# The last half tile of a mixture-of-experts layer as float32 products in two column halves, and the tokens' products without their split

## The chip, the cores and the metric

The program runs on one core of a Trainium2 chip. The metric is the device time of one execution in microseconds (us). TensorE is called PE here, its weight loads PEld, VectorE DVE, ScalarE ACT, GpSimd POOL, and SyncE, which issues most DMAs, SP.

## The reference

Eight batches of 576 tokens go through an attention with 32 memory slots per head, and the result through a layer with eight experts, of which each token uses the one with the highest score.

```python
a = softmax(phi); k_m = a^T k; v_m = a^T v              # 8 batches, 8 heads, 576 tokens, 32 slots, 64 wide
x = softmax(q k_m^T / 8) v_m                            # tokens: [4608, 512]
expert = argmax(norm(x) @ norm(expert_emb).T / tau)     # one of 8
gate = softmax(logits)[expert]
out[token] = gate * (relu(x @ w1[expert]) @ w2[expert]) # 512 -> 1024 -> 512, float32
```

## The kernel before

Float32 accuracy is wanted. A product of two float32 operands that is to run in PE's quick format (float32r) is written as three: each operand is split into a high part and the rest, and high*high, high*low and low*high are added in PSUM. Names ending in h and l are such parts: `wh`, `wl` of the second layer's weights, `gh`, `gl` of the first layer's, `hh`, `hl` of the hidden activations, `vh`, `vl` of the tokens' value weights, and the two `aT` tiles of a batch's transposed attention weights. Other matmuls (`acc`, `pg`, `ts`, `tl`) run on unsplit float32.

A batch nearly always has one expert for all its tokens; `batch(b)` assumes that of the batch's chosen expert, and `rest` handles the other tokens, of which there are none here. `batch(b)` runs the first layer (`first`: 2 halves of 288 tokens by 8 blocks of hidden units, six matmuls each into a PSUM tile `ph` of which there are four buffers, tag "mm", shared with `py`, `pg` and one `tl`) and the second (`second`: tiles of 128 tokens at T0 = 0, 128, 256, 384, 448, 24 matmuls of 512 columns each into `py`). 576 is four and a half times 128, so the fifth tile overlaps the fourth by 64 rows, and only its last 64 rows are written out. After each `ph`, ACT writes `hh` and DVE writes `hl`; between them ACT and DVE split the next weights (`split_w`, with `wl` mostly on POOL).

While `batch(b)` runs, the attention of batch b+1 is woven in between its matmuls: `weigh` (scores transposed, `sc`, then softmax on DVE and ACT), `divide`, `turn` (weights transposed back, `ta`, and split into `aT`), `attend` (the tokens' products with `vh` and `vl` into `po`, with logits beside them), `choose` (the batch's expert, `key`), and then `late`: flags, norms and gates, some 26 small DVE operations and an exponential on ACT. Where a step stands is decided while the program is written, by `run`: it keeps planned times of PE, DVE and ACT (`plan`), and lets a step go once its inputs are due and neither DVE nor ACT is planned more than `slack` ahead of PE. The engines then work through their own instructions in the order written. `choose` also sets the loads of w1 and w2 going on SP, since only then the expert is known.

Batch 0's attention has nothing to be woven into; it is written out by hand at the start (`moe_linformer`) and is followed by batch 1's `te`, `acc`, `tf`, `ts`, `tl` and then `project(0)` (`pg`, `gh`, `gl`) and `first(0)`.

Of the kernel before, what the change touches and what calls it, by code (L numbers as in the profile page):

```python
# [26 lines left out]
T0 = (0, 128, 256, 384, 448)  # L27
# [21 lines left out]
class Tokens:  # L49
# [43 lines left out]
    def turn(self, p):  # L93
        k, nc, b = self.k, self.nc, self.b
        ah, al = k.aT[b % 2]
# [5 lines left out]
        o = 0 if p < 2 else 64  # L101
        g, to = slice(gs[0], gs[-1] + 1), slice(T0[ti[0]] + o, T0[ti[-1]] + P)
        nc.scalar.copy(ah[:, g, to], t[:, :, o:])
        nc.vector.tensor_tensor(out=al[:, g, to], in0=t[:, :, o:], in1=ah[:, g, to].bitcast(F32), op=ALU.subtract)  # L104
        n = 4 if p < 2 else 1
        pe = k.plan("PE", 0.11 * max(n, 2))
        k.end["aT", b, p] = k.plan("DVE", 0.15 + 0.135 * n, k.plan("ACT", 0.2 + 0.1 * n, pe))

    def attend(self, *ti, pt=None):

        k, nc, b = self.k, self.nc, self.b
        ah, al = k.aT[b % 2]
        for i in ti:
            self.po[i] = po = (pt or self.pt)([P, NC * (D + E)], f"po{b}_{i}")
            to = slice(T0[i], T0[i] + P)
            for g in range(NG):
                w = slice(g * (P + E), (g + 1) * (P + E))
# [13 lines left out]
        k.end["po", b, ti[-1]] = k.plan("DVE", 0.35 + 0.18 * len(ti), pe)  # L131
# [86 lines left out]
    def steps(self):  # L218

        k, b = self.k, self.b  # L220
        end = k.end

        def past():

            return b - 2 < k.halved
# [30 lines left out]
class Kernel:  # L256
# [4 lines left out]
    def __init__(self, ctx, tc, phiT, qT, kv, kvt, emb, tau, w1, w2, out):  # L261
# [10 lines left out]
        self.ad = dp.tile([B, P, 2, NG * S], F32, name="ad")  # L272
# [10 lines left out]
        self.sT = st([P, NG, S], F32, name="sT")  # L283
# [3 lines left out]
        self.vh = st([P, NG * (P + E)], F32R, name="vh")  # L287
        self.vl = st([P, NG * (P + E)], F32R, name="vl")
# [3 lines left out]
        self.aT = [[st([P, NG, S], F32R, name=f"aT{i}{k}") for k in range(2)] for i in range(2)]  # L292
# [9 lines left out]
        self.hl = st([P, 8, S], F32R, name="hl")  # L302

# [8 lines left out]
        self.chosen, self.n1, self.n2, self.projected, self.halved, self.halves = set(), 0, 0, 0, -1, 0  # L312
        self.left = None
# [5 lines left out]
    def consts(self):  # L319
# [15 lines left out]
        for x in (self.vh, self.vl):  # L335
            nc.vector.tensor_scalar(
                out=x, in0=self.ident[:, :1].broadcast_to((P, NG * (P + E))), scalar1=0.0, scalar2=None, op0=ALU.mult
            )
# [164 lines left out]
    def scores(self, b, pt, gs=range(NG), products=True):  # L503
# [27 lines left out]
        for g in gs:  # L531
            nc.scalar.copy(self.sT[:, g, 512:], tail[g][:, :64])
            self.plan("ACT", 0.22)
# [3 lines left out]
    def products(self, b):  # L537

        nc = self.nc
        parts = [  # L540
            (slice(64 * k, 64 * k + 64), self.tail[g], slice((P + E) * g + 64 * k, (P + E) * g + 64 * k + D + E))
            for g in range(NG)
            for k in range(2)
        ]
        for h, x, to in parts:
            nc.scalar.copy(self.vh[h, to], x[h, 64:])
            act = self.plan("ACT", 0.23)
        for h, x, to in parts:
            nc.vector.tensor_tensor(out=self.vl[h, to], in0=x[h, 64:], in1=self.vh[h, to].bitcast(F32), op=ALU.subtract)
            self.end["v", b] = self.plan("DVE", 0.24, act)  # L550


    def keep(self, b):

        for k, x in enumerate(self.aT[b % 2]):
            self.nc.sync.dma_start(self.ad[b, :, k], x.rearrange("p g s -> p (g s)").bitcast(F32))
        self.nc.sync.dma_start(self.vd[b].rearrange("p (g k m) -> p g k m", g=NG, k=2), self.vT[b % 2][..., :D])
# [16 lines left out]


# [34 lines left out]
    def first(self, n, at, split):  # L610

        nc = self.nc
        gh, gl, (ah, al) = self.gh, self.gl, at
        free = [0.0] * 4
        for s in range(2):
            to = slice(s * HS, s * HS + HS)
            for f in range(8):
# [11 lines left out]
                free.append(self.plan("DVE", 0.46, self.plan("ACT", 0.42, self.plan("PE", 0.79, free[-4]))))  # L629
# [3 lines left out]
    def second(self, n, gate, put, split):  # L633

        nc = self.nc
        for i in range(NT):
            to = slice(T0[i], T0[i] + P)
            p = self.mm([P, DM], f"py{n}_{i}")
            for f in range(8):
                split(f)  # L640
                for k, (h, w) in enumerate(((self.hh, self.wh), (self.hh, self.wl), (self.hl, self.wh))):
                    nc.tensor.matmul(p, lhsT=h[:, f, to], rhs=w[:, f], start=f == 0 and k == 0, stop=f == 7 and k == 2)  # L642
                pe = self.plan("PE", 0.69)
# [3 lines left out]
            nc.scalar.activation(y, p, AF.Copy, scale=gate[:, i : i + 1])  # L647
            self.plan("ACT", 0.7, pe)
            put(i, y)
            yield  # L650
# [48 lines left out]
    def batch(self, b, attention):  # L699
# [16 lines left out]
        for _ in self.first(b, self.aT[b % 2], split):  # L716
            self.run(attention)
        while self.halves < 8:
            self.split_w(b == 0)
        self.halved = b + 1  # L720
        self.late = True
        self.loads()
        for n, _ in enumerate(self.second(b, self.gate[:, b], self.rows(b), must)):
            if n == 5:
                self.run(attention, lambda: ("gate", b) in self.end)
                if b == B - 1:
                    self.left = self.others()
            self.hold = n >= 16 and b + 1 < B
# [14 lines left out]
    def rows(self, b):  # L743
        def put(i, y):
            o = 0 if i < 4 else 64
            r = b * S + T0[i]
            self.nc.gpsimd.dma_start(self.out[r + o : r + P], y[o:])  # L747
# [13 lines left out]
    def rest(self, fl, ni):  # L761
# [3 lines left out]
        with tc.If(nv > 0, preferred_fallthrough_block=False):  # L765
# [29 lines left out]
            for i in range(NT):  # L795
                nc.gpsimd.iota(
                    tok[:, i : i + 1], pattern=[[0, 1]], base=T0[i], channel_multiplier=1, allow_small_or_imprecise_dtypes=True
                )
            gate = st([P, NT], F32, name="g1")
            ex = st([P, NT], F32, name="e1")  # L800
            ix = st([P, NT], I32, name="ix")
            at, vT = self.aT[0], self.vT[0]

            def put(i, y):
                nc.gpsimd.indirect_dma_start(
                    out=self.out,
                    out_offset=bass.IndirectOffsetOnAxis(ap=ix[:, i : i + 1], axis=0),
                    in_=y,
                    in_offset=None,
                    bounds_check=N - 1,  # L810
# [3 lines left out]
            with tc.For_i(0, nv, 1) as j:  # L814
                b = nc.sync.value_load(tab[:, 0, bass.ds(j, 1)], min_val=0, max_val=B - 1)
                e = nc.sync.value_load(tab[:, 1, bass.ds(j, 1)], min_val=0, max_val=E - 1)
                for k in range(2):
                    nc.sync.dma_start(
                        at[k].rearrange("p g s -> p (g s)").bitcast(F32),
                        self.ad[bass.ds(b, 1), :, k].rearrange("a p s -> (a p) s"),  # L820
                    )
# [7 lines left out]
                bc = st([P, 1], F32, name="bc")  # L829
                nc.vector.tensor_copy(out=ec, in_=ef[:, bass.ds(j, 1)])  # L830
# [3 lines left out]
                nc.vector.scalar_tensor_tensor(out=ix, in0=tok, scalar=bc, in1=ex, op0=ALU.add, op1=ALU.add)  # L834
# [8 lines left out]
                for _ in self.first("r", at, split):  # L843
# [112 lines left out]
```

## Time and profile before

| | |
|---|---|
| median of 3 runs | 481.5 us (479.58 to 481.68) |
| the profiled execution | 479.94 us |
| its span, first to last instruction | 478.1 us |
| PE busy | 451.0 us, 94% |
| DVE, ACT, POOL busy | 262.5, 196.6, 100.4 us |
| mean granted PE clock | 0.978 |

Busy time is the time in which at least one instruction of an engine was under way. Matmuls overlap each other, so the mean duration of one is not what one costs: that is the spacing of their starts, or the length of a row of them divided by their count. The chain of waits goes back from the last instruction, at each step to what released it; read in order of time it tells which engine's work set the end at each moment. "x40" counts instructions as the chip ran them; an unsplit float32 matmul stands there as two (20 `acc` matmuls of the program are x40 in the trace). The granted clock has two levels, 1.00 (2.4 GHz) and 0.50 (1.2 GHz).

### The profile page before, as it was taken

How to read it: one execution, taken by the hardware profiler on the slowest of the kernel's cores; microseconds unless marked ns; L12 is line 12 of the kernel's file. 1: busy time of each engine (PE TensorE's matmuls, PEld its weight loads, DVE VectorE, ACT ScalarE, POOL GpSimd, SP SyncE). 2: the span in 40 equal slices, each digit the busy share in tenths (PEclk: the TensorE clock that was granted, in tenths of full speed). 3: DMA queues.
4: the chain of work that ended last, by engine and by line, in shares of the span. 5: the costliest groups of instructions: out<-in, count | busy, mean ns of one | idle time of the engine just before them, and what ended most of it. 6: DMA issues, size and time to landing. Idle time of an engine off the chain costs nothing.

```text
span 478.1 us, 9454 instructions
## 1 busy us (share of the span) xinstructions
PE 451.0 (94%) x3604; PEld 375.1 (78%) x3604; DVE 262.5 (55%) x875; ACT 196.6 (41%) x479; POOL 100.4 (21%) x108
## 2 busy tenths in 40 slices
PE   3858899999999999999999999999999999999993
PEld 2446598879887798879988798878988798869882
DVE  5463698456846467536856368446756367437100
ACT  4332563157414573137514473236623383126210
POOL 1000041004400170004400071004400062015300
PEclk9966999999999999999999999999999999999998
DMA  8644891199316970299215970199414900094011
GB/s 287 221 186 185 256 368 47 32 347 348 141 45 264 349 254 22 62 385 347 96 45 224 374 268 22 40 344 350 156 44 182 337 2 23 22 338 179 25 45 36
DMA packets 26321, 87.18 MB, mean 182 GB/s; under 512 B 7064, under 2 KB 7064, under 8 KB 24224
## 3 DMA queue, kind: packets, MB, share of 16 engines
q1 hardware_dynamic: 23216, 76.82, 45.1%
q0 software_dynamic: 2944, 9.44, 5.1%
q8 instruction: 30, 0.49, 0.4%
q10 hardware_dynamic: 112, 0.28, 0.2%
q14 instruction: 19, 0.16, 0.1%
HBM read 66.60 MB, written 19.92 MB: 181 GB/s over the span
## 4 chain that ended last, share of the span: by engine, by line
PE 85%; issue 6%; DVE 3%; DMA 2%; POOL 1%; ACT 1%; POOLq 0%; DVEq 0%; ACTq 0%
PE py L642 41%; PE ph L622 21%; PE po L119 6%; PE acc L463 4%; PE pg L600 3%; PE ts L509 2%; PE te L450 2%; PE sc L72 2%; PE ta L100 2%; DMA kx<-kv 1%; DMA kl<-kvt 1%; POOL wl L589 1%; POOL out_dram L747 0%; PE tf_0False L489 0%; PE tl L520 0%
## 5 line engine op out<-in xcount | busy, mean ns | idle before, releaser
L642 PE MATMUL py<-wh,hh 128*128 128x512 f32 x320 | 129.7, 405 | 0.0
L642 PE MATMUL py<-wh,hl 128*128 128x512 f32 x320 | 125.2, 391 | 0.0
L642 PE MATMUL py<-wl,hh 128*128 128x512 f32 x320 | 125.1, 391 | 0.0
L622 PE MATMUL ph<-aT,gh 128*128 128x288 f32 x512 | 104.7, 299 | 1.8 <-DVE gl L604 1.8
L589 POOL TENSOR_TENSOR wl<-w2s,wh 128x512 fp32r<-128x512 f32 x60 | 76.6, 1291 | 122.4 <-ACT wh L580 115.8
L622 PEld LDWEIGHTS ph<-aT,gh 128*128 128x128 f32 x512 | 81.3, 188 | 5.8 <-DVE gl L604 4.8
L647 ACT ACTIVATE ys<-py,gate 128x512 f32<-128x512 f32 x40 | 27.5, 687 | 126.2 <-PE py L642 103.7
L622 PE MATMUL ph<-aT,gl 128*128 128x288 f32 x256 | 75.3, 294 | 0.0
L747 POOL DMA_DIRECT2D out_dram<-ys x40 | 22.1, 552 | 248.9 <-ACT ys L647 165.5
L626 DVE SCALAR_TENSOR_TENSOR hl<-ph,hh 128x288 fp32r<-128x288 f32 x128 | 56.1, 453 | 29.5 <-ACT hh L625 29.1
L642 PEld LDWEIGHTS py<-wh,hl 128*128 128x128 f32 x320 | 60.1, 188 | 13.3
L642 PEld LDWEIGHTS py<-wh,hh 128*128 128x128 f32 x320 | 60.2, 188 | 11.7 <-issue 1.2
L642 PEld LDWEIGHTS py<-wl,hh 128*128 128x128 f32 x320 | 60.3, 188 | 10.3
L625 ACT ACTIVATE hh<-ph 128x288 fp32r<-128x288 f32 x128 | 50.8, 413 | 25.6 <-PE ph L622 25.5
L622 PEld LDWEIGHTS ph<-aT,gl 128*128 128x128 f32 x256 | 48.0, 188 | 0.0
L604 DVE TENSOR_TENSOR gl<-pg,gh 128x512 fp32r<-128x512 f32 x32 | 19.9, 683 | 47.2 <-ACT gh L603 47.2
L119 PE MATMUL po<-vh,aT 128*128 128x136 f32 x160 | 30.1, 287 | 0.8 <-DVE aT L104 0.8
L580 ACT CAST wh<-w2s 128x512 fp32r<-128x512 f32 x50 | 30.5, 614 | 0.0
L119 PEld LDWEIGHTS po<-vh,aT 128*128 128x128 f32 x160 | 28.3, 208 | 2.8 <-DVE aT L104 1.0
L125 DVE TENSOR_REDUCE lg<-po 128x8 f32<-128x16 f32 x40 | 7.0, 175 | 40.6 <-PE po L119 40.6
L119 PE MATMUL po<-vl,aT 128*128 128x136 f32 x80 | 23.3, 291 | 0.0
L77 ACT ACTIVATE ea<-ea 128x512 f32<-128x512 f32 (+1 forms) x24 | 13.4, 560 | 22.4 <-DVE ea L76 22.3
(122 smaller groups left out, 490.8 us busy)
## 6 DMA issues: line engine op xcount, KB each, us to landing
kx<-kv SPq DMA_DIRECT2D x32, 512.0 KB, 7.8
w1s<-w SPq DMA_DIRECT2D x16, 1024.0 KB, 5.4
w2s<-w SPq DMA_DIRECT2D x32, 512.0 KB, 9.1
ad<-aT SPq DMA_DIRECT2D x16, 576.0 KB, 13.0
out_dram<-ys POOLq DMA_DIRECT2D x32, 256.0 KB, 2.3
qt<-qT SPq DMA_DIRECT2D x14, 576.0 KB, 6.4
ex<-phiT SPq DMA_DIRECT2D x16, 288.0 KB, 11.1
kl<-kvt SPq DMA_DIRECT2D x7, 256.0 KB, 8.4
```

The source lines that it names most:

```text
L119: nc.tensor.matmul(po[:, 144 * g : 144 * g + P + E], lhsT=x[:, g, to], rhs=v[:, w], start=n == 0, stop=n == 2)
L463: nc.tensor.matmul(self.acc[32 * i : 32 * i + 32, i], lhsT=self.eT[:, 5 * g + k, 32 * j : 32 * j + 32], rhs=src[:, 4 * g + j], start=k == ...
L580: nc.scalar.copy(h, x)
L589: nc.gpsimd.tensor_tensor(out=l, in0=x, in1=h.bitcast(F32), op=ALU.subtract)
L600: nc.tensor.matmul(ps[g][j], lhsT=vT[r, g, c % 2, i], rhs=self.w1s[r, c, f], start=True, stop=True)
L604: nc.vector.tensor_tensor(out=self.gl[:, g, f], in0=ps[g], in1=self.gh[:, g, f].bitcast(F32), op=ALU.subtract)
L622: nc.tensor.matmul(p, lhsT=w[:, g, fs], rhs=x[:, g, to], start=g == 0 and k == 0, stop=g == 1 and k == 2)
L625: nc.scalar.activation(self.hh[:, f, to], p, AF.Relu)
L626: nc.vector.scalar_tensor_tensor(out=self.hl[:, f, to], in0=p, scalar=0.0, in1=self.hh[:, f, to].bitcast(F32), op0=ALU.max, op1=ALU.subtract)
L642: nc.tensor.matmul(p, lhsT=h[:, f, to], rhs=w[:, f], start=f == 0 and k == 0, stop=f == 7 and k == 2)
L647: nc.scalar.activation(y, p, AF.Copy, scale=gate[:, i : i + 1])
L747: self.nc.gpsimd.dma_start(self.out[r + o : r + P], y[o:])
```

## The change

Four things are changed. The fifth tile holds the last 64 tokens alone. It is computed first in `second`, from unsplit float32: `h4`, a new copy of those 64 tokens' activations that ACT writes in `first` after `hh` and `hl`, is the stationary operand (64 columns of the array), and w2's unsplit columns 0 to 255 go to the array's lower 64 columns and 256 to 511 to its upper 64, as two matmuls of 256 columns. The tokens' products are one float32 matmul each, from `aw` (the unsplit transposed weights) and `vv`. The split into `aT`, still needed by `first`, is made from `aw` by DVE and POOL (`part`), in one pair of tiles and no longer two; `turn` of batch b+1 may therefore come only after `first` of batch b. w2 of the next batch may be loaded once the half tile is computed, and no longer before `second`.

```diff
-T0 = (0, 128, 256, 384, 448)
+T0 = (0, 128, 256, 384, 512)
@@ turn
-        nc.scalar.copy(ah[:, g, to], t[:, :, o:])
-        nc.vector.tensor_tensor(out=al[:, g, to], in0=t[:, :, o:], in1=ah[:, g, to].bitcast(F32), op=ALU.subtract)
...
+        a = k.aw[:, g, to]
+        nc.scalar.copy(a, t)
...
+        k.part(g, slice(to.start, min(to.stop, S)))
@@ attend
-                for n, (x, v) in enumerate(((ah, k.vh), (al, k.vh), (ah, k.vl))):
-                    nc.tensor.matmul(
-                        po[:, 144 * g : 144 * g + P + E], lhsT=x[:, g, to], rhs=v[:, w], start=n == 0, stop=n == 2
-                    )
-            pe = k.plan("PE", 0.68)
+                nc.tensor.matmul(po[:, 144 * g : 144 * g + P + E], lhsT=k.aw[:, g, to], rhs=k.vv[:, g], start=True, stop=True)
+            pe = k.plan("PE", 0.5)
@@ products
+                if g:
+                    self.nc.vector.tensor_copy(out=to, in_=x)
+                else:
+                    self.nc.scalar.copy(to, x)
@@ part (new)
+        self.nc.vector.tensor_copy(out=ah, in_=a)
+        self.nc.gpsimd.tensor_tensor(out=al, in0=a, in1=ah.bitcast(F32), op=ALU.subtract)
@@ first, after hh and hl
+                if s:
+                    nc.scalar.activation(self.h4[:, f], p[:, HS - 64 :], AF.Relu)
+                    free[-1] = max(free[-1], self.plan("ACT", 0.21))
@@ second
-        for i in range(NT):
+        for i in (NT - 1, *range(NT - 1)):
+            half = i == NT - 1
...
+                if half:
+                    for j in range(2):
+                        nc.tensor.matmul(
+                            p[64 * j : 64 * j + 64],
+                            lhsT=self.h4[:, f],
+                            rhs=self.w2s[:, f, d * j : d * j + d],
+                            start=f == 0,
+                            stop=f == 7,
+                        )
...
```

The order of three engines shows where this stands. On PE, the end of `first` and the start of `second` in batch 3, with the scores `sc` of batch 4 between them; before:

```order
L622 MATMUL ph3_17_2761<-aT10_87,gl_95 128x288
L642 MATMUL py3_0_2772<-wh_92,hh_96 128x512
L642 MATMUL py3_0_2772<-wl_93,hh_96 128x512
L642 MATMUL py3_0_2772<-wh_92,hl_97 128x512
L72 MATMUL sc4_0_2776<-ident_116,sT_79 128x128 x4
...
```

and changed:

```order
L623 MATMUL ph3_17_2677<-aT0_84,gl_93 128x288
L649 MATMUL py3_4_2689<-w2s_89,h4_96 64x256 x2
L73 MATMUL sc4_0_2692<-ident_115,sT_79 128x128 x4
L73 MATMUL sc4_1_2701<-ident_115,sT_79 128x128 x4
L73 MATMUL sc4_2_2710<-ident_115,sT_79 128x128 x2
L649 MATMUL py3_4_2689<-w2s_89,h4_96 64x256 x14
L660 MATMUL py3_0_2735<-wh_90,hh_94 128x512
...
```

Sixteen matmuls of the half tile stand where the first tile of 24 began, and the scores go in after the first two of them.

On ACT, the second half of `first` in batch 3, with what each row waits for; before:

```order
L625 ACTIVATE hh_96<-ph3_11_2701 128x288 [waits PE_49]
L580 CAST wh_92<-w2s_91 128x512 [waits DMAHW6_49,Pool_49]
L625 ACTIVATE hh_96<-ph3_12_2712 128x288 [waits PE_49]
L625 ACTIVATE hh_96<-ph3_13_2721 128x288 [waits PE_49]
L625 ACTIVATE hh_96<-ph3_14_2732 128x288 [waits PE_49]
```

and changed:

```order
L626 ACTIVATE hh_94<-ph3_11_2611 128x288 [waits PE_49]
L633 ACTIVATE h4_96<-ph3_11_2611 128x64 [waits DVE_49]
L581 CAST wh_90<-w2s_89 128x512 [waits DMAHW3_49,Pool_49]
L626 ACTIVATE hh_94<-ph3_12_2623 128x288 [waits PE_49]
L633 ACTIVATE h4_96<-ph3_12_2623 128x64 [waits DVE_49]
L626 ACTIVATE hh_94<-ph3_13_2633 128x288 [waits PE_49]
```

Each `hh` is followed by an `h4` that waits for DVE: for the `hl` of the same `ph`, the other reader of that PSUM tile.

On DVE, at the start of the program, what stands between batch 1's products (`vl`, now `vv`) and the first `gl` of batch 0; before:

```order
L549 TENSOR_TENSOR vl<-tl_01_537,vh 64x72 x2
L171 TENSOR_REDUCE cm_593<-key_416 128x1
L172 TENSOR_SCALAR own_594<-key_416,cm_593 128x8
L173 SCALAR_TENSOR_TENSOR fl<-key_416,own_594 128x8
L181 TENSOR_SCALAR ss_184<-ss_184 128x5
L40 TENSOR_SCALAR nrg<-ss_184 128x5
L41 TENSOR_SCALAR nrg<-nrg 128x5
L44 RECIPROCAL nrr<-nrg 128x5
L45 SCALAR_TENSOR_TENSOR nrr<-nrr,ss_184 128x5
L46 SCALAR_TENSOR_TENSOR nrg<-nrg,nrr 128x5
L604 TENSOR_TENSOR gl<-pg_00_607,gh 128x512
```

and changed, from the last of these nine small operations on:

```order
L47 SCALAR_TENSOR_TENSOR nrg<-nrg,nrr 128x5
L45 RECIPROCAL nrr<-nrg 128x5
...
L47 SCALAR_TENSOR_TENSOR n_570<-nrg,nrr 128x5
L179 TENSOR_SCALAR n_570<-n_570 128x5
L180 RECIPROCAL n_570<-n_570 128x5
...
L195 TENSOR_TENSOR l_587<-l_587,m_183 128x40
...
L205 TENSOR_REDUCE zz_596<-l_587 128x5
L206 TENSOR_SCALAR zz_596<-zz_596 128x5
L207 RECIPROCAL gate<-zz_596 128x5
L605 TENSOR_TENSOR gl<-pg_00_600,gh 128x512
```

Seventeen more small operations of batch 0's `late` (the rest of the root, and the gates) now stand ahead of the first `gl`, and on ACT the gates' exponential stands ahead of the first `gh`.

## Rows read from the trace of the kernel before

**Rows 1.** The page: span and busy time of each engine.

```profile
span 478.1 us, 9454 instructions
PE 451.0 (94%) x3604; PEld 375.1 (78%) x3604; DVE 262.5 (55%) x875; ACT 196.6 (41%) x479; POOL 100.4 (21%) x108
```

**Rows 2.** Windows, one batch: us, busy PE, PEld, DVE, ACT, POOL, clock, DMA, GB/s.

```profile
213.45:267.85 54.40, 54.40 (x458) 45.86 (x465) 31.73 (x106) 24.04 (x59) 12.96 (x13) 1.00 0.55 201
```

**Rows 3.** The chain of waits in that batch: start us, us, what.

```profile
213.45 1.89 PE pg L600 x32
215.34 1.23 PE acc L463 x40
...
225.77 5.82 PE ph L622 x42
...
233.37 8.18 PE py L642 x36
241.55 1.09 PE ta L100 x10
...
244.70 1.29 PE po L119 x12
```

**Rows 4.** Timeline of PE, a change of shape: start us, us, what.

```profile
210.43 0.48 PE L642 MATMUL py<-wh,hh 128*128 128x512 f32 x1
210.75 0.40 PE L642 MATMUL py<-wl,hh 128*128 128x512 f32 x1
```

**Rows 5.** Timeline of ACT in the first layer of that batch.

```profile
219.58 0.62 ACT L580 CAST wh<-w2s 128x512 fp32r<-128x512 f32 x1
220.09 1.07 ACT L625 ACTIVATE hh<-ph 128x288 fp32r<-128x288 f32 x3
...
226.34 0.35 ACT L532 COPY sT<-tl 128x64 f32<-128x64 f32 x2
...
227.49 0.41 ACT L625 ACTIVATE hh<-ph 128x288 fp32r<-128x288 f32 x1
...
231.62 0.41 ACT L625 ACTIVATE hh<-ph 128x288 fp32r<-128x288 f32 x1 [0.37 <-PE ph L622]
```

**Rows 6.** Timeline of DVE, end of that first layer and the softmax.

```profile
232.07 0.46 DVE L626 SCALAR_TENSOR_TENSOR hl<-ph,hh 128x288 fp32r<-128x288 f32 x1 [0.32 <-ACT hh L625]
232.75 0.69 DVE L75 TENSOR_REDUCE mx<-sc 128x16 f32<-128x512 f32 x1 [0.23 <-PE sc L72]
...
240.72 0.42 DVE L90 TENSOR_TENSOR ea<-ea,z 128x256 f32<-128x256 f32 x1
```

**Rows 7.** Groups by line and shape: weight loads of the second layer.

```profile
L642 PEld LDWEIGHTS py<-wl,hh 128*128 128x128 f32 x320 | 60.3, 188 | 10.3
```

**Rows 8.** Timeline of PE at the start, batch 0's attention.

```profile
29.17 1.08 PE L100 MATMUL ta<-ident,ea 128*128 128x128 f32 x4 [3.58 <-issue]
...
30.83 0.66 PE L119 MATMUL po<-vh,aT 128*128 128x136 f32 x2
...
38.15 0.41 PE L119 MATMUL po<-vl,aT 128*128 128x136 f32 x1
```

**Rows 9.** Windows at the start (columns as in rows 2).

```profile
26.00:28.00 2.00, 0.00 (x0) 0.00 (x0) 1.41 (x3) 1.93 (x8) 0.00 (x0) 0.78 1.03 418
...
44.00:46.00 2.00, 1.53 (x26) 0.90 (x28) 0.18 (x1) 1.17 (x4) 0.00 (x0) 0.96 0.98 414
```

**Rows 10.** The chain of waits from the products of batch 1 to `ph`.

```profile
52.22 0.23 DVE vl L549
...
54.23 0.61 DVE gl L604
...
54.89 2.11 PE ph L622 x14
```

**Rows 11.** Timeline of DVE, the seventeen small operations in a later batch: first, last.

```profile
258.17 0.19 DVE L44 RECIPROCAL nrr<-nrg 128x5 f32<-128x5 f32 x1
...
261.79 0.19 DVE L213 RECIPROCAL gate<-zz 128x5 f32<-128x5 f32 x1
```

More of the change, by code (lines that the diff above doesn't have):

```diff
@@ L26 @@
 NC = 4
-T0 = (0, 128, 256, 384, 448)
+T0 = (0, 128, 256, 384, 512)
+S2 = S + 64
 NT = len(T0)
@@ L223, in past @@
         def past():
-            return b - 2 < k.halved
+            return b - 1 < k.hidden
         def each(step):
@@ L291, in __init__ @@
         self.step, self.slack, self.hold, self.late = None, 1.0, False, False
-        self.aT = [[st([P, NG, S], F32R, name=f"aT{i}{k}") for k in range(2)] for i in range(2)]
+        self.aT = [st([P, NG, S], F32R, name=f"aT{k}") for k in range(2)]
+        self.aw = st([P, NG, S2], F32, name="aw")
         self.acc = self.ps.tile([P, 4, 2 * D], F32, name="acc")
@@ L312, in __init__ @@
         self.chosen, self.n1, self.n2, self.projected, self.halved, self.halves = set(), 0, 0, 0, -1, 0
+        self.hidden = 0
         self.left = None
@@ L334, in consts @@
         nc.vector.tensor_scalar(out=self.eb, in0=self.i8, scalar1=1.0 / (E * P), scalar2=None, op0=ALU.mult)
[L335 to L338, printed above, removed]
+        nc.vector.memset(self.vv, 0.0)
         nc.gpsimd.memset(self.kl[64:], 0.0)
@@ L531, in scores @@
         for g in gs:
-            nc.scalar.copy(self.sT[:, g, 512:], tail[g][:, :64])
+            nc.scalar.copy(
+                self.sT[:, g, 512:].rearrange("p (k s) -> p k s", k=2),
+                tail[g][:, :64].unsqueeze(1).broadcast_to((P, 2, 64)),
+            )
             self.plan("ACT", 0.22)
@@ L537, in products @@
     def products(self, b):
[L539 to L550, printed above, removed]
+        for g in range(NG):
+            for k in range(2):
+                h = slice(64 * k, 64 * k + 64)
+                x, to = self.tail[g][h, 64:], self.vv[h, g, 64 * k : 64 * k + D + E]
+                if g:
+                    self.nc.vector.tensor_copy(out=to, in_=x)
+                else:
+                    self.nc.scalar.copy(to, x)
+                t = self.plan("DVE" if g else "ACT", 0.23)
+                self.end["v", b] = max(self.end.get(("v", b), 0.0), t)
     def keep(self, b):
-        for k, x in enumerate(self.aT[b % 2]):
-            self.nc.sync.dma_start(self.ad[b, :, k], x.rearrange("p g s -> p (g s)").bitcast(F32))
+        self.nc.sync.dma_start(self.ad[b], self.aw[..., :S])
         self.nc.sync.dma_start(self.vd[b].rearrange("p (g k m) -> p g k m", g=NG, k=2), self.vT[b % 2][..., :D])
@@ L573, in loads, with part @@
             self.n2 += 1
+    def part(self, g, to):
+        ah, al = (x[:, g, to] for x in self.aT)
+        a = self.aw[:, g, to]
+        self.nc.vector.tensor_copy(out=ah, in_=a)
+        self.nc.gpsimd.tensor_tensor(out=al, in0=a, in1=ah.bitcast(F32), op=ALU.subtract)
+        self.plan("DVE", 0.15 + a.shape[1] * a.shape[2] / 950)
     def split_w(self, hurry=False):
@@ L608, in project, with first @@
             yield
-    def first(self, n, at, split):
+    def first(self, n, split):
         nc = self.nc
-        gh, gl, (ah, al) = self.gh, self.gl, at
+        gh, gl, (ah, al) = self.gh, self.gl, self.aT
         free = [0.0] * 4
@@ L628, in first @@
                 )
-                free.append(self.plan("DVE", 0.46, self.plan("ACT", 0.42, self.plan("PE", 0.79, free[-4]))))
+                pe = self.plan("PE", 0.79, free[-4])
+                free.append(self.plan("DVE", 0.46, self.plan("ACT", 0.42, pe)))
+                if s:
+                    nc.scalar.activation(self.h4[:, f], p[:, HS - 64 :], AF.Relu)
+                    free[-1] = max(free[-1], self.plan("ACT", 0.21))
                 split(8 * s + f)
@@ L635, in second @@
         nc = self.nc
-        for i in range(NT):
-            to = slice(T0[i], T0[i] + P)
-            p = self.mm([P, DM], f"py{n}_{i}")
+        for i in (NT - 1, *range(NT - 1)):
+            half = i == NT - 1
+            d = DM // 2 if half else DM
+            p = self.mm([P, d], f"py{n}_{i}")
             for f in range(8):
[L640 to L643, printed above, removed]
+                if half:
[6 more added lines that the diff above has]
+                            stop=f == 7,
+                        )
+                else:
+                    split(f)
+                    to = slice(T0[i], T0[i] + P)
+                    for k, (h, w) in enumerate(((self.hh, self.wh), (self.hh, self.wl), (self.hl, self.wh))):
+                        nc.tensor.matmul(
+                            p, lhsT=h[:, f, to], rhs=w[:, f], start=f == 0 and k == 0, stop=f == 7 and k == 2
+                        )
+                pe = self.plan("PE", 0.44 if half else 0.69)
                 if f < 7:
@@ L646, in second @@
             y = self.wk.tile([P, DM], F32, tag="ys", name=f"ys{n}_{i}", bufs=3)
-            nc.scalar.activation(y, p, AF.Copy, scale=gate[:, i : i + 1])
-            self.plan("ACT", 0.7, pe)
+            nc.scalar.activation(y[:, :d], p, AF.Copy, scale=gate[:, i : i + 1])
+            self.plan("ACT", 0.45 if half else 0.7, pe)
             put(i, y)
@@ L715, in batch @@
         self.slack = 1.8
-        for _ in self.first(b, self.aT[b % 2], split):
+        for _ in self.first(b, split):
             self.run(attention)
+        self.hidden = b + 1
         while self.halves < 8:
             self.split_w(b == 0)
-        self.halved = b + 1
         self.late = True
-        self.loads()
         for n, _ in enumerate(self.second(b, self.gate[:, b], self.rows(b), must)):
@@ L727, in batch @@
                     self.left = self.others()
+            if n == 7:
+                self.halved = b + 1
+                self.loads()
             self.hold = n >= 16 and b + 1 < B
@@ L744, in put @@
         def put(i, y):
-            o = 0 if i < 4 else 64
             r = b * S + T0[i]
-            self.nc.gpsimd.dma_start(self.out[r + o : r + P], y[o:])
+            if i < NT - 1:
+                self.nc.gpsimd.dma_start(self.out[r : r + P], y)
+            else:
+                for j in range(2):
+                    h = slice(256 * j, 256 * j + 256)
+                    self.nc.gpsimd.dma_start(self.out[r : r + 64, h], y[64 * j : 64 * j + 64, :256])
         return put
@@ L798, in rest @@
                 )
+            t4 = tok[:, NT - 1 :]
+            nc.vector.tensor_scalar(out=t4, in0=t4, scalar1=2.0, scalar2=None, op0=ALU.mult)
+            nc.vector.tensor_scalar(out=t4[64:], in0=t4[64:], scalar1=-127.0, scalar2=None, op0=ALU.add)
             gate = st([P, NT], F32, name="g1")
@@ L816, in rest @@
                 e = nc.sync.value_load(tab[:, 1, bass.ds(j, 1)], min_val=0, max_val=E - 1)
[L817 to L821, printed above, removed]
+                nc.sync.dma_start(self.aw[..., :S], self.ad[bass.ds(b, 1)].rearrange("a p g s -> (a p) g s"))
                 nc.sync.dma_start(vT[..., :D], self.vd[bass.ds(b, 1)].rearrange("a p (g k m) -> (a p) g k m", g=NG, k=2))
@@ L833, in rest @@
                 nc.vector.tensor_scalar(out=ex, in0=ex, scalar1=ec, scalar2=OOB, op0=ALU.not_equal, op1=ALU.mult)
-                nc.vector.scalar_tensor_tensor(out=ix, in0=tok, scalar=bc, in1=ex, op0=ALU.add, op1=ALU.add)
+                for i, f in ((slice(0, NT - 1), 1.0), (slice(NT - 1, NT), 2.0)):
+                    nc.vector.tensor_scalar(out=b2, in0=bc, scalar1=f, scalar2=None, op0=ALU.mult)
+                    nc.vector.scalar_tensor_tensor(
+                        out=ix[:, i], in0=tok[:, i], scalar=b2, in1=ex[:, i], op0=ALU.add, op1=ALU.add
+                    )
+                self.part(slice(0, NG), slice(0, S))
                 for _ in self.project("r", vT):
@@ L841, in split @@
                         self.split_w()
-                for _ in self.first("r", at, split):
+                for _ in self.first("r", split):
                     pass
```

29 lines of the change are left out of this document (13 added, 16 removed).

## The prediction

> **What bounds the kernel now.** I read the page first: PE is busy for 451.0 of 478.1 us [rows 1]. Then the windows: in one batch of the middle PE is busy for all of its 54.40 us at full clock, DVE for 31.73 and ACT for 24.04, and DMA takes 0.55 of its share [rows 2]. Then the chain of waits in that batch, which is one run of matmuls with no other engine in it [rows 3]. So PE's own work sets the end from batch 1 to batch 7, and a microsecond of matmuls taken away there is one gained unless PE then waits. At the start it is otherwise: there DVE's queue stands in the chain between `pg` and `ph` [rows 10].
>
> **The half tile.** It removes 24 matmuls a batch. 36 of them take 8.18 us [rows 3], 0.227 each, so 5.45 us. It adds 16 unsplit ones of 256 columns, two rows each in the trace, in two column halves, so 16 rounds of a pair. The nearest rows are `acc` (four column strips side by side, 128 columns: 40 rows in 1.23 us, 10 rounds of 0.123) and `pg` (eight tiles side by side, 512 columns: 32 rows in 1.89 us, four rounds of 0.472) [rows 3]. On the line through both, 256 columns cost 0.24 a round, 3.8 us a batch. The bounds: 3.7 if only the line's slope of 0.91 ns a column counted, 7.6 if the two halves ran one after the other. I take 3.8, since both rows show tiles side by side. That is -1.65 a batch, -13.2 in all.
>
> **Changes of shape.** A `py` matmul after transposes is followed by the next 0.32 us later [rows 4] and not 0.227, so a change costs about 0.1. The half tile adds three a batch (in from `ph`, and out and in around the scores or out to `py`): +0.3, +2.4 in all; bounds 0 and twice that.
>
> **The wait of `h4`.** In the second half of `first` ACT must now do `hh`, wait for DVE's `hl` of the same tile, do `h4`, and only then the next `hh`. A turn, from rows: `hl` starts 0.45 after `hh` and takes 0.46 [rows 5, 6]; `h4` is as large as a tail copy, two of which take 0.35, so 0.18 until ACT takes the next, with 0.04 for the handover: 1.13 us. With a weight split in between it is 0.51 more (219.58 to 220.09 [rows 5]). PE needs 5.82/7 = 0.83 a tile [rows 3]. So ACT, which had time to spare, falls behind by 0.3 a tile and by 0.8 where it splits. PE feels it through the four buffers: a tile can start when the one four places earlier is released, now 1.18 after its `hh` (0.45+0.46+0.04, and 0.23 for the whole of `h4`, my estimate from the two tail copies). I follow it on the clock of rows 5: `hh` of tile 11 at 227.1 (227.49, less two of the four `vh` copies gone), tiles 12, 13 and 14 at 228.74, 229.87 and 231.0, their releases at 229.92, 231.05 and 232.18. Tile 16 starts at 229.97, 17 at 231.1 and the half tile at 232.23, where PE would have been ready at 231.6: 0.6 lost. The last `h4` (tile 17) ends at 236.1, and the half tile, with the scores in it, wants it at 236.9, so no more is lost there. The softmax starts after the last `hl`, at 235.8 and not 232.75; it lasts 8.4 [rows 6], and its first transposes are wanted near 243.6, when two of the three groups are ready and the third just so. +0.6 in batches 0 to 6. In batch 7 no scores stand in the half tile to give ACT time; I put 1.1 there. In all +5.3; bounds 0 (if the release were early enough) and 1.4 a batch.
>
> **The tokens' products.** In a batch of the middle 12 matmuls take 1.29 us [rows 3], so 30 take 3.2. In their place 10 unsplit ones, 20 rows of 136 columns; at `acc`'s 0.123 for 128 columns, 0.131 each, 2.6 us. No row shows an unsplit matmul with weights for all 128 columns; the bounds are 0.107 a row (what a row costs now, 1.29/12: 2.1) and 0.32 (a load of 0.188 [rows 7] not hidden: 6.4). I take 2.6, as a `py` row with the same load of 0.188 comes every 0.227 while its 512 columns stream, so loads are hidden. -0.58 for seven batches, -4.1.
>
> The Trainium skill says otherwise ("TensorE: Matmul & The Clock Gate", part 3 on row and column tiling, "The mechanism"): a weight load runs beside a matmul in flight only where the two use different row groups. All of these use all rows, so load and stream would add up. The rows do not agree: 0.188 for the load and 0.227 from start to start leave no room for both. By the rule the products would take 6.4 a batch and each half tile 3 us more.
>
> **The rest of a batch.** DVE loses its subtraction from PSUM and gets a copy, POOL gets three subtractions, ACT a larger third copy; none is in the chain, and POOL is busy for 13 of 54 us [rows 2]. These are wanted at the next `first`, some 20 us later: nothing. w2's load still waits for `choose`, which comes after the half tile; one DMA of `ad` fewer: nothing, bounds half a microsecond either way a batch.
>
> **The start.** Batch 0's products run at half clock, from 30.83 to 38.4 (38.15 and the spacing of one [rows 8]), with a wait for the DVE split in them. Now 20 rows at 0.26: 5.2 us, and no split to wait for. -2.3. After that the chain goes through DVE: four `vl` of 0.23 [rows 10] become two `vv`, which start two ACT copies of that length earlier: -0.9. But seventeen more small operations stand before the first `gl`. In a later batch the same ones last from 258.17 to 261.98 [rows 11], 3.8 us with their wait for ACT. `first(0)` cannot start before `gl`, and nothing else is there for PE. So +0.6 at the start, in place of a gain of 3.2.
>
> **The sum.** -13.2 + 2.4 + 5.3 - 4.1 + 0.6 = -9.0. The profiled execution's 479.94 becomes 470.9. The median of the runs shown lies 1.6 above that execution, so I predict 472. The tail is taken as it is, though the last tile written is now a whole one.
>
> **Rivals.**
> *The halves do not run side by side* (slower). Place: the 16 rounds in each batch. 7.6 in place of 3.8, +30, gives 502. It decides from 4.9 us a half tile on, where the gain of 9.0 is used up. For it: no row shows strips of 64 columns. Against it: strips of 32 and tiles of 64 rows do run side by side [rows 3]. 7%.
> *`h4` costs more*: if the next `hh` starts only after `h4` has ended, a turn is 1.28, the half tile starts at 232.7 and the softmax comes too late for the transposes by 0.3: 1.4 a batch, 478. For it: all of this turn is waits between engines, which I priced from rows without this pattern. 18%.
> *The clock rises early*: the split products did not raise it, it was down at 26 to 28 and up again only after `te` and `acc` of batch 1, at 44 to 46 [rows 9]. The new products stream as `acc` does and could raise it during batch 0's products; then the rest of them and `te`, `acc`, `tf` would take some 3 to 5 us less: 468. Against it: the wait before `first(0)` grows to some 4 us, and after one of 3.58 [rows 8] the clock was down [rows 9]; lost again, it costs about 1.5. 15%.
> *Loads are not hidden*: 3.8 more for the products in seven batches (6.4 in place of 2.6) and 16 loads of 0.188 [rows 7] more for each half tile, +51: 523. Against it stand the 0.227 of `py`. 2%. It is the Trainium skill's rule of above.
> That the change takes no PE work away can be excluded: the rows of the order are fewer by the count above.
>
> **How the numbers follow.** My forecast has 58%, with its own range of 467 to 477. What can be told from no change is 0.5%, 2.4 us. Faster: the forecast nearly whole, the early clock and a third of the `h4` case, 0.79. Same: most of the other `h4` outcomes, 0.10. Slower: the halves, the loads and the worst of `h4` with a late clock, 0.11. The range goes from 463 (the early clock with little wait) to 481 (the costly `h4`).
>
> **What would show it.** The half tile's 32 rows should last 3.8 us beside the scores; 7 or more means the first rival. On ACT, `hh` to `hh` in the second half of `first` should be about 1.13 and 1.6 with a split, and PE should have short waits before tiles 16 and 17 and before the half tile, put down to ACT. `po` should take 0.26 a product. Before `first(0)` PE should idle for about 4 us with DVE's small operations as the chain. I am wrong if a batch in the middle is not between 52.2 and 53.8 us long (54.4 - 1.65 + 0.3 + 0.6 - 0.58 = 53.1), or if a wait for w1 or w2 appears in the chain.

## The result and the profile after

The changed kernel takes 469.17 us, median of 4 runs (467.85 to 470.05), beside 481.59 of the kernel before (479.58 to 481.7, 4 runs): a ratio of 0.977 with a 95% interval of 0.974 to 0.980. The forecast was 472 (463 to 481), faster. Its profiled execution took 467.85 beside 479.94, so the trace has 12.1 us to explain where the sum had 9.0.

The page after: span and busy time by engine.

```profile
span 466.0 us, 9511 instructions
...
PE 433.3 (93%) x3588; PEld 347.6 (75%) x3588; DVE 263.7 (57%) x858; ACT 204.0 (44%) x527; POOL 130.1 (28%) x140
```

TensorE's work fell by 17.7 us [rows 1], the span by 12.1. The windows of the same batch in the middle, to be held against [rows 2]: window, then busy time of PE, PEld, DVE, ACT, POOL, granted clock, DMA share, GB/s.

```profile
208.23:260.83 52.60, 52.60 (x456) 42.54 (x463) 32.16 (x104) 24.97 (x65) 16.71 (x17) 1.00 0.55 197
```

It is 1.80 shorter, and PE is still busy throughout. The chain of waits in it, which answers to [rows 3] (start, us, what):

```profile
220.55 6.30 PE ph L623 x42
226.85 0.64 PE py L649 x4
227.49 1.24 PE sc L73 x10
228.74 3.17 PE py L649 x28
...
240.74 0.93 PE po L115 x8
...
246.76 0.46 PE po L115 x4
```

L649 is the half tile: 0.64 + 3.17 = 3.81. `ph` has grown from 5.82 to 6.30, `po` is 2.32 in a batch (0.93, 0.93, 0.46). Where the 1.80 comes from, all rows of the chain added up by name for this batch:

| us in the batch | before | after | difference |
|---|---|---|---|
| second layer (120 rows of `py`; after 96, and 32 of the half tile) | 27.96 | 22.61 + 3.81 | -1.54 |
| first layer `ph` | 13.13 | 13.62 | +0.49 |
| scores `sc`, now inside the half tile | 1.09 | 1.24 | +0.15 |
| products `po` | 3.20 | 2.32 | -0.88 |
| all else | 9.0 | 9.0 | 0 |

The timeline of ACT in the first layer's second half, to be held against [rows 5]; the bracket is the idle time before an instruction and what ended it.

```profile
223.53 0.41 ACT L626 ACTIVATE hh<-ph 128x288 fp32r<-128x288 f32 x1
224.47 0.22 ACT L633 ACTIVATE h<-ph 128x64 f32<-128x64 f32 x1 [0.52 <-DVE hl L627]
224.59 0.41 ACT L626 ACTIVATE hh<-ph 128x288 fp32r<-128x288 f32 x1
225.52 0.22 ACT L633 ACTIVATE h<-ph 128x64 f32<-128x64 f32 x1 [0.53 <-DVE hl L627]
```

Each `h4` (named h in the trace) waits half a microsecond for `hl`, and the next `hh` stands behind it: a turn of 1.06.

By stage the span's 12.1 divide so, from the first `pg` of each batch on PE: up to batch 0 -6.35 (50.43 to 44.08); batch 0 +3.55; batch 1 -0.55; batches 2 to 6 -9.23 together (269.13 to 259.90); from the last `pg` on about +0.5. So the middle gave 9.8, the two ends together 2.3. Of the 6.35, 0.92 is an earlier start of batch 0's products in this execution (30.83 to 29.91; in the fourteen traces they start between 29.9 and 33.4); from the first of them to `pg` it is 19.61 before and 14.17 after. Batch 1 gave 0.55 and not 1.8: `acc` no longer stands between its `pg` and its `ph`, so that PE waits 0.53 there for `gl`, and two transposes (`tf`) have moved into it from the end of batch 0. In batch 0 the wait from `pg` to `ph` grew from 4.46 to 7.26, the first layer from 13.29 to 17.00, and the rest shrank by 2.97: the second layer begins at 68.34 where it had begun at 68.18. PE at the start, and the windows around it (columns as above):

```profile
29.91 4.04 PE L115 MATMUL po<-vv,aw 128*128 128x136 f32 x20
...
51.34 0.85 PE L623 MATMUL ph<-aT,gh 128*128 128x288 f32 x2 [4.48 <-DVE gl L605]
```

```profile
30.00:32.00 2.00, 2.00 (x11) 2.00 (x11) 1.15 (x5) 1.23 (x3) 1.11 (x1) 0.50 0.00 0
32.00:34.00 2.00, 2.00 (x15) 1.92 (x15) 1.12 (x7) 0.00 (x0) 0.57 (x2) 0.73 0.00 0
34.00:36.00 2.00, 1.19 (x11) 0.91 (x10) 1.60 (x12) 0.59 (x1) 0.00 (x0) 1.00 0.00 0
48.00:50.00 2.00, 0.00 (x0) 0.00 (x0) 1.72 (x11) 0.29 (x2) 0.00 (x0) 1.00 1.00 352
50.00:52.00 2.00, 0.66 (x3) 0.66 (x4) 1.91 (x7) 2.00 (x4) 0.00 (x0) 0.54 1.06 375
52.00:54.00 2.00, 2.00 (x10) 2.00 (x10) 1.45 (x3) 0.41 (x1) 0.00 (x0) 0.50 0.98 201
54.00:56.00 2.00, 2.00 (x10) 2.00 (x10) 0.55 (x2) 0.92 (x2) 0.38 (x1) 0.50 1.02 352
56.00:58.00 2.00, 2.00 (x14) 2.00 (x13) 0.67 (x2) 1.07 (x3) 0.90 (x1) 0.76 1.04 416
```

The granted clock rises from 0.50 (1.2 GHz) to 1.00 (2.4 GHz) during the new products, some ten microseconds earlier than before [rows 9]. PE then stands idle for 4.48 us, and the first layer begins at 0.50. In the kernel before, the split products keep PE just as busy, and the clock stays down:

```profile
34.00:36.00 2.00, 2.00 (x11) 2.00 (x11) 0.52 (x3) 0.00 (x0) 0.00 (x0) 0.50 0.00 0
```

### The profile page after: what moved, and what is told of

It is laid out like the page before. It is cut to its first block, busy times and chain, and to the rows that moved or that the text cites. A ratio compares the mean times of both kernels' runs of the same rounds, so it can differ in the third digit from the quotient of the medians.

```text
span 466.0 us, 9511 instructions
## 1 busy us (share of the span) xinstructions
PE 433.3 (93%) x3588; PEld 347.6 (75%) x3588; DVE 263.7 (57%) x858; ACT 204.0 (44%) x527; POOL 130.1 (28%) x140
## 4 chain that ended last, share of the span: by engine, by line
PE 81%; issue 6%; DVE 5%; ACT 3%; DMA 2%; POOL 1%; POOLq 0%; DVEq 0%; ACTq 0%
PE py L660 34%; PE ph L623 21%; PE py L649 6%; PE acc L456 4%; PE po L115 4%; PE pg L601 2%; PE sc L73 2%; PE ts L502 2%; PE ta L100 2%; PE te L443 2%; DMA kx<-kv 1%; DMA kl<-kvt 1%; POOL wl L590 1%; DVE hl L627 1%; ACT hh L626 1%
## 5 line engine op out<-in xcount | busy, mean ns | idle before, releaser
L660 PE MATMUL py<-wh,hh 128*128 128x512 f32 x256 | 105.8, 413 | 0.0
L660 PE MATMUL py<-wh,hl 128*128 128x512 f32 x256 | 100.4, 392 | 0.0
L660 PE MATMUL py<-wl,hh 128*128 128x512 f32 x256 | 100.0, 391 | 0.0
L667 ACT ACTIVATE ys<-py,gate 128x512 f32<-128x512 f32 (+1 forms) x40 | 25.6, 641 | 90.4 <-issue 55.1
L770 POOL DMA_DIRECT2D out_dram<-ys x32 | 17.7, 552 | 155.7 <-ACT ys L667 104.0
L660 PEld LDWEIGHTS py<-wh,hh 128*128 128x128 f32 x256 | 48.1, 188 | 12.3 <-DVE ea L77 2.3
L574 POOL TENSOR_TENSOR aT<-aw,aT 128x512 fp32r<-128x512 f32 (+1 forms) x24 | 25.4, 1081 | 33.9 <-DVE aT L573 33.9
L649 PE MATMUL py<-w2s,h 128*64 128x256 f32 x256 | 31.2, 386 | 1.2 <-ACT h L633 1.2
L633 ACT ACTIVATE h<-ph 128x64 f32<-128x64 f32 x64 | 14.3, 223 | 34.2 <-DVE hl L627 34.2
L649 PEld LDWEIGHTS py<-w2s,h 128*64 128x64 f32 x256 | 16.9, 136 | 11.6 <-ACT h L633 3.7
L115 PEld LDWEIGHTS po<-vv,aw 128*128 128x128 f32 x160 | 23.3, 203 | 1.8
## 6 DMA issues: line engine op xcount, KB each, us to landing
ad<-aw SPq DMA_DIRECT2D x8, 576.0 KB, 12.1
```

The costliest lines, as they stand in the source:

```text
L115: nc.tensor.matmul(po[:, 144 * g : 144 * g + P + E], lhsT=k.aw[:, g, to], rhs=k.vv[:, g], start=True, stop=True)
L574: self.nc.gpsimd.tensor_tensor(out=al, in0=a, in1=ah.bitcast(F32), op=ALU.subtract)
L649: nc.tensor.matmul(p[64 * j : 64 * j + 64], lhsT=self.h4[:, f], rhs=self.w2s[:, f, d * j : d * j + d], start=f == 0, stop=f == 7,)
L667: nc.scalar.activation(y[:, :d], p, AF.Copy, scale=gate[:, i : i + 1])
```

## Experiments

The theory after this reading: (a) the half tile gives 1.54 a batch and loses 0.49 of it to ScalarE's wait; (b) the products give 0.88; (c) at the start the gain of 6.35 is lost, in equal parts, to `gl` behind the small operations and to a first layer that is slow because the clock has fallen again. The rivals are with each run. Ratios are to the kernel before (478 to 482 beside each). Where not said otherwise the edit is made in the changed kernel. Start times differ by up to 3 us between executions (the first `pg` comes at 44.1 to 47.1 in the eleven traces with unsplit products), so batch 0 is compared from its first `pg` on.

### One part without the other

```
 second(): for i in range(NT): three split products each, last tile from token 448
 first():  no h4
```

> The changed kernel with its last half tile put back: five tiles of 24 split products in the second layer, no unsplit copy of the layer's input; tokens' products stay unsplit. If the parts add: against the changed kernel the half tile costs 5.45 in place of 3.81 in each batch and the 0.48 of waits behind the copy goes, so about +1.2 in each of six batches, less at both ends: 476 to 477, with a middle batch of about 53.8 and po still 2.3 in it. If the half tile in unsplit float32 gives nothing: 469.

472.02 (ratio 0.984, 0.981 to 0.986), between the two: the half tile as it stands is worth 3 us and not 7. From the chain of a middle batch, 53.40 long:

```profile
222.84 5.79 PE ph L623 x42
228.62 0.71 PE py L646 x3
229.33 1.09 PE sc L73 x10
```

So `ph` without the copy is 5.79, and `sc`, with the same duplicated shapes, is 1.09: the 0.15 is not of the shapes but of standing inside the half tile. `py` is 27.88 in this kernel, so the half tile takes 1.46 off it, loses 0.51 in `ph` and 0.15 in `sc`, and nets 0.80 a batch.

```
-    nc.tensor.matmul(po[...], lhsT=k.aw[:, g, to], rhs=k.vv[:, g], ...)
+    for n, (x, v) in enumerate(((aT[0], vh), (aT[1], vh), (aT[0], vl))): ...
```

> The changed kernel with its tokens' products put back to three split ones of each pair; the half tile stays unsplit. If the parts add: po costs 3.2 in place of 2.32 in seven batches, +6.2: 475 to 476, and where the clock at the start stays low as before, pg of the first batch begins at about 50 and the 17 small VectorE operations ahead of gl cost another 2 to 3: 478. Middle batch about 53.5. If it is the unsplit products that raise the clock early, the granted clock at 34 to 36 us is 0.50 here; if something else in the change does, it is 1.00 and pg begins before 46.

490.8 (ratio 1.024, 1.020 to 1.028): far outside what was expected, slower than before. The clock part held: with PE busy throughout it is 0.50 at 34 to 36 us, so the split products do not raise it and the unsplit ones do.

```profile
34.00:36.00 2.00, 2.00 (x11) 2.00 (x11) 0.52 (x3) 0.00 (x0) 0.00 (x0) 0.50 0.00 0
```

But a middle batch was 55.1, and its chain ran through ScalarE:

```profile
233.17 0.31 ACT hh L629
233.50 0.47 DVE hl L630
234.00 0.22 ACT h L636
234.22 0.31 ACT hh L629
```

Tile after tile at 1.05, while PE needs 0.8. The planner, which counts other times for split products, had put `ts`, `tl` and their copies behind the first layer and not into it, and with them went a pause of 1.4 us in PE's first layer, in which ScalarE can catch up. That the missing pause is what made the chain is a reading of it; no run moves these steps alone. `w1` also came late at the first and the last change of batch (8.2 and 8.0 us in the chain). This suggested the run with the copy on GpSimd, which is the last one below.

### Do the two halves run side by side?

```
-    for j in range(2):
-        nc.tensor.matmul(p[64*j : 64*j+64], lhsT=h4[:, f], rhs=w2s[:, f, d*j : d*j+d], ...)
+    nc.tensor.matmul(p[:64], lhsT=h4[:, f], rhs=w2s[:, f], ...)
```

> The half tile as 8 products of 64 tokens by 512 columns in one half of the array's columns, in place of 8 pairs of 64 by 256 in both halves. If the pair ran side by side: 16 rows of 512 columns at 0.472 (as pg) are 7.6 in place of 3.8, +3.7 in each of eight batches: 499. If the two halves already ran one after the other: no change, 469.

496.31 in one run, a middle batch of 55.97 in place of 52.60. Its half tile in the chain:

```profile
240.03 1.05 PE py L648 x2
241.08 1.24 PE sc L73 x10
242.32 6.15 PE py L648 x14
```

7.20 in place of 3.81, 0.45 a row of 512 columns. Side by side is worth 3.4 a batch; without it the changed kernel is slower than the kernel before.

### The clock at the start

```
+    p = self.pt([P, 512], "fill")
+    for _ in range(10): nc.tensor.matmul(p, lhsT=ident, rhs=sT[:, 0, :512], ...)
     self.projected = 1
```

> Ten products of 128 by 512 whose result nobody reads, between pg and ph of the first batch, where TensorE waits 4.5 us for gl. If it is the clock lost in that wait that makes the first layer of this batch slow: granted clock near 1.0 from 52 on, first layer about 14 in place of 17, py at 65.5 in place of 68.3: 466. If the first layer is slow by its waits for the splits and copies alone: 469 or a little more.

470.82 (ratio 0.981, 0.977 to 0.985), not the 466 expected: a product is two rows in the trace, and the ten took 8.78 us, twice the wait that they were to fill, so `ph` was pushed back by 3.7 (11.00 behind `pg` in place of 7.26). The clock stayed at 1.00, and the first layer took 14.77 (56.67 to 71.44) and not 17.00. With five:

> Five products that nobody reads between pg and ph of the first batch: 4.4 us by the 0.878 that each took in the run with ten, beside a wait of 4.5 for gl. Clock alone: ph begins as in the changed kernel, 7.3 behind pg, the first layer takes 14.2 as with ten and not 17.0, py begins 21.5 behind pg in place of 24.3: 466 to 467. If a filled wait does nothing by itself: 469.

466.57 (ratio 0.972, 0.968 to 0.976). The chain and the windows:

```profile
45.27 2.58 PE pg L601 x32
47.84 4.49 PE fill L726 x10
52.33 6.60 PE ph L623 x48
...
66.81 1.95 PE py L649 x16
```

```profile
52.00:54.00 2.00, 2.00 (x13) 1.67 (x13) 2.00 (x5) 1.40 (x4) 0.00 (x0) 1.00 1.05 305
```

Products that nobody reads, put into a wait of the same length (`pg` to `ph` 7.27 as against 7.26), make the first layer 2.5 us shorter: 14.48 in place of 17.00. That the clock falls in the wait costs 2.5 us here.

### The small operations ahead of `gl`

```
-    k.run(attention)                      # before the first batch, and inside project(0)
+    elif f % 2: self.one(attention)       # first(0): one step after every second tile
```

> The changed kernel with the first batch's 26 small VectorE operations (norms and gates of its tokens) no longer ahead of gl but spread, one step after every second tile of the first layer; the rest of the program keeps its order. If the start's gain is lost to gl waiting behind them and to the clock that falls meanwhile: ph begins about 1.5 after the last pg, near 48 in place of 51.3, at a granted clock of 1.0, the first layer of this batch takes 14.2 to 15 in place of 17.0, py begins at 62 to 63.5 in place of 68.3, and the whole is 464. If py there waits for the second layer's weights or their splits instead: 467 to 469.

466.97 (ratio 0.972, 0.968 to 0.976). `ph` begins 2.80 after `pg` in place of 7.26, at full clock, as expected, but the first layer then takes 16.70: half of the gain came back as a new chain. From it:

```profile
53.32 0.69 DVE wl L587
54.01 0.09 DVE ss L175
...
54.51 0.72 DVE hl L627 x2
...
58.69 0.22 ACT h L633
58.91 0.31 ACT hh L626
59.25 0.47 DVE hl L627
```

VectorE is full: `hl`, half of the `wl` and the small operations, and from 58.7 on the copies of ScalarE behind `hl`.

### The copy's place

```
+    if s: nc.scalar.activation(self.h4[:, f], p[:, HS - 64 :], AF.Relu)
     nc.vector.scalar_tensor_tensor(out=self.hl[:, f, to], ...)
-    if s: nc.scalar.activation(self.h4[:, f], p[:, HS - 64 :], AF.Relu)
```

> The changed kernel with the unsplit copy issued ahead of hl, right behind hh: ScalarE no longer stands still 0.5 us for VectorE in each of 8 tiles. If ScalarE's wait for hl is what makes ph late: ph of a middle batch's second half back from 6.30 to 5.8, middle batch 52.1 in place of 52.6, total 464 to 465. If the chain hh, copy, hl, each waiting for the one before, holds the tile as long as the chain hh, hl, copy did (now 0.41 + 0.22 + 0.46 and two hand-overs): 52.5 and 468 to 469.

462.57 (ratio 0.961, 0.957 to 0.966), with a middle batch of 52.01. ScalarE's timeline:

```profile
223.59 0.26 ACT L628 ACTIVATE h<-ph 128x64 f32<-128x64 f32 x1
224.05 0.41 ACT L626 ACTIVATE hh<-ph 128x288 fp32r<-128x288 f32 x1 [0.20 <-PE ph L623]
224.36 0.22 ACT L628 ACTIVATE h<-ph 128x64 f32<-128x64 f32 x1
224.85 0.41 ACT L626 ACTIVATE hh<-ph 128x288 fp32r<-128x288 f32 x1 [0.27 <-PE ph L623]
```

Now ScalarE waits for PE, and a turn is PE's 0.80. The rival, that the chain of three holds the tile as long in either order, is refuted: what counts is who stands still in it.

```
+    x, y = (h[:, f, S - 64 :].bitcast(F32) for h in (self.hh, self.hl))
+    nc.gpsimd.tensor_tensor(out=self.h4[:, f], in0=x, in1=y, op=ALU.add)
```

> The changed kernel with the unsplit copy made by GpSimd as hh + hl, out of SBUF, so that neither ScalarE nor the PSUM tile has anything to do with it. If the copy is the whole of the 0.5: ph of the second half is 5.8 as before the change, middle batch 52.1, total about 464. If something else in that stretch is the cause: 6.3 and 469. If GpSimd, with eight more operations between its eight splits of 1.28, is late: a wait of py for h4 at the half tile, over 470.

462.08 (ratio 0.961, 0.957 to 0.966). Its chain in a middle batch of 51.99:

```profile
218.06 5.79 PE ph L623 x42
223.86 0.58 PE py L649 x4
224.44 1.24 PE sc L73 x10
225.68 3.17 PE py L649 x28
```

`ph` is 5.79 again, as without any copy, and the half tile loses nothing to GpSimd. The copy's wait was the whole of the 0.5, and another 0.06 in the half tile. Not all of this run's 7 us is the copy's: batch 1 is 51.99 as well, because the planner, which no longer counts the copy, has `acc` between `pg` and `ph` again. In the run with the copy ahead of `hl`, where the order of the other steps is that of the changed kernel, batch 1 is 53.26.

### The end

```
-    for i in (NT - 1, *range(NT - 1)):
+    for i in range(NT) if n == B - 1 else (NT - 1, *range(NT - 1)):
```

> The changed kernel with the half tile last instead of first in the last batch alone, so that the last store is of 64 rows and the half tile does not wait for its copies there. If both cost what the trace says (about 1.0 at the end, 0.4 to 1.1 at the half tile): 1.0 to 2.0 less, 467 to 468. If the end is a store whose length does not count: 469.

468.76 (ratio 0.975, 0.971 to 0.979): not to be told from the changed kernel. The last stage has two parts. From the last batch's first `pg` until the last store is given out, it is 43.77 before (428.04 to 471.81) and 43.25 in the changed kernel (415.46 to 458.71), and 42.15 to 42.26 in the four runs with the copy on GpSimd or ahead of `hl`: the copy behind `hl` costs 1.1 here. After the last store is given out, the span goes on for 6.3 before (to 478.1), for 7.3 in the changed kernel (to 466.0) and for 7.4 here, where that store is a quarter of a tile; but for 6.2 in the run with one half, whose last store is a whole tile. So the size of the last store does not decide, and this last 1.0 stays without a shown cause.

### Both repairs, and the half tile alone once more

The spread operations of the first batch, with the copy on GpSimd and with the copy ahead of `hl`:

> The small VectorE operations of the first batch spread and the unsplit copy made by GpSimd, together. If both gains stand side by side: 2.2 for the start from one and 7 for the copy from the other, 459 to 460. If the start without the copy is bound by VectorE or by the second layer's weights anyway: 462, as with the copy alone.

> The same two, but with the copy on ScalarE ahead of hl in place of GpSimd: 459 to 460 if the place of the copy is all the same once ScalarE does not wait, 461 to 462 if ScalarE is short in the first batch, where it also casts the weights.

458.57 (ratio 0.955, 0.952 to 0.958) and 456.85 (0.951, 0.948 to 0.955), 6 runs each: 4.9% under the kernel before, better than the changed one by 2.6%. The gains stand side by side and a little more. In batch 0 the first layer takes 15.21 with GpSimd's copy and 14.22 with ScalarE's, so that ScalarE is not short there; but the two totals' intervals overlap.

> The half tile with split tokens' products once more, the copy on GpSimd in place of ScalarE. If it is the copy's chain on ScalarE that made that kernel slower than before: no ACT in the chain of a middle batch, which is then 52.0 and 0.88 for po, 52.9, and the whole 468 to 470. If the order of the steps with split products is at fault, with w1's load behind them: 480 or more.

472.48 (ratio 0.982, 0.978 to 0.987), a middle batch of 53.1. It is the kernel of 490.8 with one operation of 64 columns moved, whose cost the planner then leaves out of its reckoning, so that the steps stand as in the changed kernel. Of its chain:

```profile
222.84 5.93 PE ph L626 x42
228.77 0.58 PE py L652 x4
229.35 1.24 PE sc L73 x10
```

So the half tile alone, without the copy on ScalarE behind `hl`, is worth 1.8%. Copy and order of steps changed together here, so how the 18 us between the two kernels divide among them stays open. The expectation of 468 to 470 was low by three: the change from batch 0 to 1 and that into the last batch came out slower than the middle, with `gl` and `w1`'s load in their chains.

The first layer of batch 0, from the start of `ph` to the start of the second layer, puts the start together:

| us | clock falls in the wait | clock stays up |
|---|---|---|
| copy on ScalarE behind `hl` | 17.00 (changed kernel) | 14.48 (five products in the wait) |
| no copy there | 15.39 (products alone), 15.37 (copy on GpSimd) | 13.29 (before), 13.39 (half tile, copy on GpSimd) |

The clock costs 2.0 to 2.5, the copy 1.2 to 1.6.

## Why the prediction was right, and where it was off

*The half tile.* 3.81 was measured for the 3.8 that the line through `acc` and `pg` gave, and the run with one half shows that the pair does run side by side. Right, and for the stated reason. What it replaces was 5.35 of the 27.96 of `py` (5.45 was reckoned from [rows 3]).

*Changes of shape.* +0.15 a batch for a forecast of +0.3. The half tile's own borders cost nothing visible; the scores inside it do.

*The wait of `h4`.* +0.49 for +0.6, a turn of 1.06 for 1.13 and 1.57 for 1.64 with a split. The mechanism is as described, and both runs that take ScalarE's wait away take exactly this. In batch 0, to which the same 0.6 was given, it cost 1.2 to 1.6: there ScalarE casts more of the weights (six `wh` in this first layer, four in that of batch 3), and no products of the next scores give it a pause; this reason is read from the trace, and no run tests it alone. In the last batch, where 1.1 was forecast, it cost 1.1.

*The tokens' products.* The mis-sized term in the middle. 2.32 for 2.6: 0.116 a row and not 0.131. The price was scaled from `acc`, whose rounds of four strips cost 0.96 ns a column; a row that uses all 128 columns of weights costs 0.85 (0.116 for 136 columns here, 0.439 for 512 in the run with ten products). That is -0.88 for -0.58. With the terms before, it makes a middle batch of 52.60 where 53.1 was forecast: in batches 2 to 6 alone 2.6 of the 3.1 us that the sum lacked (9.23 gained for 5 times 1.33). The start and batch 0 gave 2.1 more than the sum had, of which 0.9 is the earlier start of that execution, and batch 1 and the end together 1.5 less. The sign that was named for a middle batch, 52.2 to 53.8, holds, and no load of w1 or w2 stands in the chain.

The rule of the Trainium skill ("TensorE: Matmul & The Clock Gate", part 3, "The mechanism"), by which a weight load runs beside a matmul only on other row groups, would have made these products 6.4, by the prediction's estimate. They use all rows, their loads are 0.190 each in the trace (the median; 0.203 is the mean, with those at half clock), and a row comes every 0.116: the loads' records overlap the rows, and one another. The measurement decides against the rule as it is put there.

*The start.* Counted from batch 0's first product, the second layer's first matmul came 1.1 later (37.35 to 38.43), and the forecast was +0.6 with another 0.6 for `h4`. But it came so by another way. The rival of the early clock came true: `pg` was 5.44 earlier (19.61 to 14.17; 13.7 to 14.2 in all eleven traces with unsplit products, 19.6 to 19.7 in the three with split ones), and with the 2.3 of the products taken off, 3.1 is left for the clock, of the 3 to 5 that this rival had. All of it was lost again. The forecast had the wait nearly right (PE idle for 4.48 in place of about 4). It had put 1.5 on the clock lost in that wait, without rows for it, where the filled wait shows 2.5, and it had priced the copy in batch 0 like one in the middle, where it costs 1.2 to 1.6. So at the start the errors cancel, which is luck; the whole time came out near the forecast because the middle did.

*The end.* With the copy's 1.1, -0.25 was forecast for the last batch, and -0.5 was measured until the last store was given out. The tail was taken as it is; 1.0 was lost there, which no term had and no run explains.

## What to carry to other kernels

A copy that reads a tile a second time should stand before the reader on the other engine, or on an engine with time to spare: not its 0.22 us but the 0.52 that its engine stands still for the other reader set the price, here about 1.5% of the whole. An edit that shortens one stage moves a wait to another place; look for what has been put, by a planner or by hand, ahead of the operation that TensorE waits for next, and reckon the granted clock as part of that wait's price. Two parts of a change need not add up when a planner places the steps: each has to be run alone before its share is told.

## What the runs showed of the hardware

- An unsplit float32 matmul of 128 rows of weights by 136 columns is two rows of 0.116 us at a granted clock of 1.00, with weight loads of 0.190 hidden, and one by 512 columns two rows of 0.439; of two halves of 64 tokens by 256 columns, side by side, 0.119 a row, and of 64 by 512 in one half 0.45.
- The unsplit products raise the granted clock from 0.50 to 1.00 while they run (33 to 34 us), where the split ones, as busy a TensorE, leave it at 0.50 to the end: 34 to 38 us in the kernel before and in both runs with split products. In all eleven traces with unsplit products it is 1.00 by 38 us.
- TensorE stood idle for 4.48 us at 46.9 to 51.3, and the clock was 0.54 at 50 to 52, 0.50 at 52 to 56 and 0.76 at 56 to 58; with ten rows in that wait whose result nobody reads it stayed at 1.00.
